# Stages that hand work from engine to engine are put further apart in a two-layer attention and GLU kernel

## The chip, the cores and the metric

The kernel runs on one core of a Trainium2 chip. The metric is the device time of one execution in microseconds; before the change its median over three runs is 2419.47 us (2416.88 to 2425.47). A core has five engines that run beside each other and wait for one another through semaphores: TensorE (PE, matrix products; PEld is its weight load), VectorE (DVE), ScalarE (ACT), GpSimd (POOL) and SyncE (SP, which here only issues DMAs). Each engine takes its instructions in the order in which the program put them in its queue.

## What is computed

One sequence of 2048 rows of 448 values passes through attention, GLU, attention, GLU, each with a layer norm ahead of it and a residual sum behind it. Attention has 16 query heads of 28 values and one shared key and value head.

```python
def _A_ref(x, wq, wk, wv, wo):
    q = (x @ wq).reshape(B, S, H, Dh).transpose(0, 2, 1, 3)
    k = x @ wk
    v = x @ wv
    scores = jnp.einsum("bhqd,bkd->bhqk", q, k) * (Dh ** -0.5)
    p = _softmax(scores, axis=-1)
    o = jnp.einsum("bhqk,bkd->bhqd", p, v)
    return o.transpose(0, 2, 1, 3).reshape(B, S, H * Dh) @ wo

def _B_ref(x, w_gate, w_up, w_down):
    h = _sigmoid(x @ w_gate) * (x @ w_up)
    return h @ w_down

x = x + _A_ref(_layernorm(x), ...)      # layer 0
x = x + _B_ref(_layernorm(x), ...)
x = x + _A_ref(_layernorm(x), ...)      # layer 1, same weights
x = x + _B_ref(_layernorm(x), ...)
```

## The kernel before

Most operands are split into two f16 parts, a high and a low one, so that products of f16 tiles keep more digits: ACT writes the high part as a cast, and DVE or POOL writes what the cast left out. Such a pair is always ACT first, then DVE or POOL.

**Units and steps.** A layer's queries are 16 units of 128 rows. A unit has 16 steps, one for each 128 keys (`kt`). One step of the loop at L904 places, by the string ORDER (L888, `XFSFSFSFSPM`): a tick of the side stages (X); four times a slice of filler work and a score product (F, then S: L494, followed by ACT's exponential P at L497); the four products with the values of the step before (P: `pv`, L505); and one group of the next unit's maxima (M). M is four products `mx` (L477), each reduced by DVE to one column (`mp`, L481). 16 such groups make a unit's row maxima (20 for layer 1's first unit), and the maxima run three groups ahead, so the last group of the next unit stands at step 12 of 16.

**The maxima's transpose.** After the last group `row_max` (L447) lets DVE make `m` (L451, L452). A later function `fin` transposes it on PE (`mt`, L457), DVE copies it (`mr`, L459), and SP stores it into a row of QS (L460), which the next unit's scores read. `fin` is deferred by LAG slices of filler (L409); four slices are a step. `defer(fn, lag)` puts a function on a list that is looked through at each slice and whenever a PSUM tile for filler is taken.

**Side stages.** `later(...)` hangs up a chain of stages, each with the number of ticks since the one before; a tick comes once in a step (X). Each finished unit runs the chain f0, fx, fy, fz, fw, fa, fb, fc (L547 to L609): the sums of the softmax go out to DRAM and come back laid out anew, DVE takes reciprocals (fy), they go out and come back copied over partitions into `lb` (fw: four DMAs of SP, L574), POOL multiplies (fa, L579), ACT and DVE split the product into `oT` (fb, L585 and L586), and fc hangs up the product with WO (L596). Then x1 and its statistics (L601), the normed row (fd: DVE `xn` L318, DVE's cast L310, POOL's low part L311 and L312), its DMA transpose (fe, L322) and ff. Two units form a block; when ff has run for both, the block's GLU work is added to the filler.

**Filler.** `bulk` (L642) is a block's GLU: seven times a gate product `gp`, tanh on ACT (`th`, L656), an up product `up`, then DVE's `th` (L664), ACT's high part of `h` (L667) and DVE's low part (L668); then the products with WD (`dn`, L693). How much filler a slice takes follows from `rate` (L927 to L931): the work left over the steps until step 48 + 32n, with n the blocks whose GLU has been added. In the last rounds of a layer (L942) a tick is followed by four slices of 450 ns of filler by the kernel's own estimate (VS, L892).

**Next layer's rows.** In layer 0, `down` makes x2 and its statistics, and then hangs up db, dc, dd, de, df: db (L709) makes the normed row with `ln_split` (DVE `xn`, ACT's cast L310, DVE's low part L311 and L312), dc transposes it by DMA, dd makes keys and values, de transposes the keys, df counts them. `xn` has one buffer, shared by fd and db.

**Banks.** `mx`, `s`, `mt` and all filler products share seven PSUM banks in rotation; PE can take a bank again only when DVE or ACT has read what was in it.

Of the kernel before, what the change touches and what calls it, by code (L numbers as in the profile page):

```python
# [8 lines left out]
F32 = mybir.dt.float32  # L9
F16 = mybir.dt.float16  # L10
I32 = mybir.dt.int32
AF = mybir.ActivationFunctionType
OP = mybir.AluOpType
# [6 lines left out]
def interleaved_layers_kernel(ctx: ExitStack, tc: tile.TileContext, x, wq, wk, wv, wo, wg, wu, wd, out, layers=2):  # L20
# [6 lines left out]
    nc = tc.nc  # L27
    _, S, D = x.shape
# [4 lines left out]
    TB, WB, HB = 2, 4, 10  # L33
# [8 lines left out]
    wk1 = ctx.enter_context(tc.tile_pool(name="wk1", bufs=2))  # L42
# [23 lines left out]
    def defer(fn, lag=0):  # L66

        pend.append((now[0] + lag, fn))
# [246 lines left out]
    def ln_split(xt, mean, r, eng=nc.vector, xn=None, hi=nc.vector.tensor_copy):  # L315
        if xn is None:
            xn = wk1.tile([128, D], F32, name="xn", bufs=1)
        nc.vector.tensor_scalar(xn, xt, mean, r, op0=OP.subtract, op1=OP.mult)  # L318
        return hilo(xn, eng, hi)
# [86 lines left out]

    QS, QH, PVS = {}, {}, {}
    stored = set()
    LAG = 4  # L409
    KEYS = {False: [0, 512, 1024, 1536, 2048], True: [0, 512, 1024, 1536, 1792, 2048]}  # L410

    def parts_of(l, u):
# [98 lines left out]


    XTQ, BLK = {}, {}
    side = []

    def later(*stages):

        side.append([stages[0][0], list(stages)])

    def tick():  # L520

        for s in list(side):
            s[0] -= 1
            if s[0] <= 0:
                flush()
                fill.run(s[1].pop(0)[1]())
                if s[1]:
                    s[0] = s[1][0][0]
                else:
                    side.remove(s)  # L530

    class Block:
# [8 lines left out]
        def tile(self, u):  # L541

            l, b = self.l, self.b
            t = u % TB
            v = {}

            def f0():  # L547
                v["o"] = PVS.pop((l, u))
                nc.sync.dma_start(sums[u % 2], v["o"][28:128:32])
                v["xr"] = wk1.tile([128, D], F32, tag="xr", name="xr", bufs=4)  # L550
                nc.sync.dma_start(v["xr"], x[0, u * 128:(u + 1) * 128] if l == 0 else x2d[u])
                return
                yield

            def fx():
                v["rc"] = wk1.tile([128, 16], F32, name="rc")
                nc.sync.dma_start(v["rc"], sums[u % 2].rearrange("g (a b) -> (g a) b", b=16))
                return
                yield

            def fy():
                nc.vector.reciprocal(v["rc"], v["rc"])
                return
                yield

            def fz():
                nc.sync.dma_start(sums[u % 2].rearrange("g (a b) -> (g a) b", b=16), v["rc"])
                return
                yield

            def fw():
                lb = v["lb"] = wk1.tile([128, 512], F32, name="lb", bufs=1)
                for g in range(G):
                    nc.sync.dma_start(lb[32 * g:32 * g + 32], sums[u % 2][g:g + 1].to_broadcast([32, 512]))  # L574
                return
                yield

            def fa():
                nc.gpsimd.tensor_tensor(v["lb"], v["o"], v["lb"], op=OP.mult)  # L579
                return  # L580
                yield

            def fb():
                oT = v["oT"] = wk1.tile([128, 2, 512], F16, name="oT")
                nc.scalar.copy(oT[:, 0], v["lb"])  # L585
                defer(lambda: nc.vector.tensor_tensor(oT[:, 1], v["lb"], oT[:, 0], op=OP.subtract))  # L586
                return
                yield

            def wo_gen():  # L590
                need(1)
                p = fps([128, D], F32, "wo")
                n = 0
                for h in range(4):
                    for a, c in ((0, 0), (0, 1), (1, 0)):
                        nc.tensor.matmul(p, v["oT"][:, a, h * 128:(h + 1) * 128], WO[:, c, h], start=n == 0, stop=n == 11)  # L596
                        n += 1
                        yield C448

                def f():  # L600
                    nc.vector.scalar_tensor_tensor(self.x1[:, t], p, osc, v["xr"], op0=OP.mult, op1=OP.add)  # L601
                    v["ls"] = ln_stats(self.x1[:, t])[0]
                defer(f)
                later((2, fd), (3, fe), (2, ff))

            def fc():
                fill.urgent.append(wo_gen())
                return
                yield  # L609

            def fd():
                if t == TB - 1:
                    self.load_w(0)
                    self.load_w(1)
                v["hl"] = ln_split(self.x1[:, t], *v["ls"], eng=nc.gpsimd)
                return
                yield

            def fe():
                if t == 0:  # L620
                    self.XT2 = wk1.tile([128, 7, TB * 128], F16, name="XT2")
                t7_dma(v["hl"], self.XT2, t)
                return
                yield

            def ff():
                self.fed += 1
                if self.fed == TB:
                    fill.add(self.bulk(), BULK)
                    if b == NBL - 1 and not self.last:  # L630
                        for n in (1, 2):
                            fill.add(qgen(l + 1, n), G * QCH)
                return
                yield
            return (1, f0), (1, fx), (1, fy), (1, fz), (1, fw), (1, fa), (1, fb), (2, fc)

        def load_w(self, f):
            need(2 + f)
# [3 lines left out]
        def bulk(self):  # L642
            l, b, XT2 = self.l, self.b, self.XT2
            hs = []

            def glu(f):
# [15 lines left out]
                def ev():  # L662
                    t = th
                    nc.vector.scalar_tensor_tensor(t, th, 1.0, up.rearrange("p j n -> p (j n)"), op0=OP.add, op1=OP.mult)  # L664

                    def parts():
                        nc.scalar.activation(h[:, 0], t, AF.Copy, scale=2.0 ** -17)  # L667
                        defer(lambda: nc.vector.scalar_tensor_tensor(h[:, 1], t, 2.0 ** -17, h[:, 0], op0=OP.mult,  # L668
                                                                     op1=OP.subtract), 1)
                    defer(parts, 2)  # L670
                defer(ev)
                hs.append(h)

# [9 lines left out]
        def down(self, t, hs):  # L683
# [23 lines left out]
            defer(ev)  # L707

            def db():  # L709
                v["hl"] = ln_split(v["x2"], *v["ls"], eng=nc.vector, hi=nc.scalar.copy)  # L710
                return
                yield

# [20 lines left out]
                yield  # L734
            if not self.last:
                v["XT"] = XTQ[l + 1, u // 4]
                later((2, db), (3, dc), (2, dd), (2, de), (2, df))

    QCH = 11 * C512
    BULK = FC * 22 * C256 + TB * 3 * FC * C448  # L740
# [144 lines left out]
        k += 1  # L885

    early[0] = False
    ORDER = "XFSFSFSFSPM"  # L888
    MORE = (5, 10)
    FIRST = KT * TB + 16  # L890
    KEEP = 28000
# [1 line left out]
    for l in range(layers):  # L893
# [10 lines left out]
        for step in range(U * KT):  # L904
            u, kt = divmod(step, KT)
            P = []
            for o in ORDER:
                if o == "S":
                    scores(l, u, kt, len(P), P)
# [63 lines left out]
```

## Time and profile before

| | |
|---|---|
| median of 3 runs | 2419.47 us |
| profiled execution | 2419.03 us, span 2417.3 us |
| granted clock of TensorE, mean | 0.978 |
| busy: PE, DVE, ACT, POOL | 2250.9, 1627.5, 1573.6, 329.0 us |
| score products `s`, `pv`, `mx` (PE) | 2048, 4096, 2064 instructions |
| exponentials P (ACT) | 2048, 1322.4 us |
| reduces mp (DVE) | 2064, 1270.9 us |

Rows of the profile read: engine, source line, operation, output <- inputs, a count or a shape. In a timeline a row begins with its start and length in us and may end with the idle time of the engine before it and what ended it. In a list of waits a row gives the engine and line that waited, what it waited for, and then the total in us, the number of times and the longest. In a table of stretches each engine has busy us and, in brackets, its instructions; behind them stand the granted clock, the DMA share and GB/s. PE's ends are modelled, so a busy PE is not PE at its peak.

### The profile page before, as it was taken

The page shows a single profiled execution, that of the slowest core. Times are in us where ns is not written, and L with a number is a line of the kernel's source. Part 1 is how long each engine was busy: PE and PEld are TensorE (multiplying, and loading weights), DVE is VectorE, ACT ScalarE, POOL GpSimd, SP SyncE. Part 2 cuts the span into 40 slices and gives each one's busy share as a digit, 9 for nine tenths or more (in the row PEclk, how much of TensorE's full clock was granted, in tenths as well). Part 3 has the DMA queues.
Part 4 walks back from the last instruction along what each step waited for, and adds up shares of the span by engine and source line. Part 5 has one row for each costly group of instructions (what it writes and reads, how often), then busy time and mean ns, then how long its engine had stood idle before and what let it go on. Part 6 is the DMA issues. An engine that isn't in the chain of part 4 may idle for free.

```text
span 2417.3 us, 40904 instructions
## 1 busy us (share of the span) xinstructions
PE 2250.9 (93%) x15608; PEld 994.7 (41%) x15608; DVE 1627.5 (67%) x2874; ACT 1573.6 (65%) x2583; POOL 329.0 (14%) x589
## 2 busy tenths in 40 slices
PE   3788899999999999999999989999999999999999
PEld 1211244343444444344564213434344444444356
DVE  3776768777767777776266987767777777767421
ACT  5386767676667767666712877767676767767751
POOL 5402546100100010001011000000000000000010
PEclk9798899999999999999999999999999999999999
DMA  5433454321223233231452011323131222322133
GB/s 144 130 100 85 148 186 138 90 88 54 86 75 101 74 90 94 59 94 47 127 155 77 13 45 59 108 57 89 51 101 61 92 74 82 91 80 84 63 100 124
DMA packets 227524, 218.57 MB, mean 90 GB/s; under 512 B 159408, under 2 KB 187760, under 8 KB 227328
## 3 DMA queue, kind: packets, MB, share of 16 engines
q1 hardware_dynamic: 221856, 200.24, 28.4%
q0 software_dynamic: 4352, 14.74, 1.7%
q8 instruction: 122, 2.00, 0.3%
q10 hardware_dynamic: 1120, 0.98, 0.1%
q14 instruction: 74, 0.61, 0.1%
HBM read 175.37 MB, written 23.59 MB: 82 GB/s over the span
## 4 chain that ended last, share of the span: by engine, by line
PE 75%; DVE 13%; DMA 3%; ACT 2%; SPq 2%; issue 2%; POOL 2%; ACTq 0%; DVEq 0%; POOLq 0%
PE pv L505 18%; PE s L494 15%; PE gp L334 10%; PE up L334 10%; DVE mp L481 10%; PE dn L693 9%; PE mx L477 6%; PE wo L596 3%; PE qp L334 2%; ACT P L497 2%; DMA XT<-hl 1%; SPq L424 1%; DMA lb<-sums 1%; SPq L574 0%; DMA wgu<-wgu_d 0%
## 5 line engine op out<-in xcount | busy, mean ns | idle before, releaser
L497 ACT ACTIVATE P<-s,esc 128x512 f32<-128x512 f32 x2048 | 1322.4, 690 | 477.2 <-PE s L494 452.6
L481 DVE TENSOR_REDUCE mp<-mx 128x1 f32<-128x512 f32 (+1 forms) x2064 | 1270.9, 679 | 468.3 <-PE mx L477 465.6
L494 PE MATMUL s<-QS,KK 96*128 96x512 f16 x2048 | 762.9, 387 | 33.4 <-DVE mp L481 23.0
L505 PE MATMUL pv<-P,VV 128*32 128x512 f32 x4096 | 558.6, 617 | 0.0
L334 PEld LDWEIGHTS <-wgu 128*128 128x128 f16 x4928 | 457.5, 97 | 239.1 <-issue 91.8
L334 PE MATMUL up<-XT,wgu 128*128 128x256 f16 x2464 | 370.6, 273 | 1.8 <-DVE mp L481 1.8
L334 PE MATMUL gp<-XT,wgu 128*128 128x256 f16 x2464 | 369.5, 274 | 2.7 <-DMA wgu<-wgu_d 2.3
L693 PE MATMUL dn<-WD,h 128*128 128x448 f16 x1344 | 319.7, 353 | 0.0
L494 PEld LDWEIGHTS <-KK 96*128 96x128 f16 x2048 | 193.7, 98 | 162.9 <-issue 82.9
L477 PE MATMUL mx<-KK,QH 32*128 32x512 f16 (+1 forms) x2064 | 232.4, 392 | 28.3 <-ACT P L497 18.1
L477 PEld LDWEIGHTS <-QH 32*128 32x128 f16 x2064 | 56.6, 91 | 454.2 <-issue 450.2
L693 PEld LDWEIGHTS <-h 128*128 128x128 f16 x1344 | 123.0, 97 | 138.5 <-issue 27.7
L579 POOL TENSOR_TENSOR lb<-pvs,lb 128x512 f32<-128x512 f32 x32 | 40.5, 1267 | 1000.5 <-DMA lb<-sums 833.1
L505 PEld LDWEIGHTS pv<-P,VV 128*32 128x32 f32 x4096 | 81.9, 109 | 205.8 <-issue 194.9
L667 ACT ACTIVATE h<-th 128x512 f16<-128x512 f32 x112 | 70.4, 628 | 93.5 <-DVE th L664 93.5
L664 DVE SCALAR_TENSOR_TENSOR th<-th,up 128x512 f32<-128x512 f32 x112 | 75.9, 678 | 63.9 <-PE up L334 51.9
L668 DVE SCALAR_TENSOR_TENSOR h<-th,h 128x512 f16<-128x512 f32 x112 | 77.0, 687 | 47.0 <-ACT h L667 47.0
L295 POOL TENSOR_SCALAR rs<-mv 128x1 f32<-128x1 f32 (+2 forms) x53 | 12.2, 230 | 676.9 <-DVE mv L290 666.1
L656 ACT ACTIVATE th<-gp,gsc 128x512 f32<-128x512 f32 x112 | 76.7, 684 | 39.8 <-PE gp L334 39.6
L334 PE MATMUL qp<-XT,WQ 128*128 128x512 f16 x352 | 100.4, 415 | 1.8 <-DVE mp L481 1.2
L596 PE MATMUL wo<-WO,oT 128*128 128x448 f16 x384 | 93.6, 355 | 0.4 <-DVE mp L481 0.4
L334 PEld LDWEIGHTS <-WQ 128*128 128x128 f16 x352 | 33.9, 104 | 54.3 <-issue 26.9
(116 smaller groups left out, 766.3 us busy)
## 6 DMA issues: line engine op xcount, KB each, us to landing
wgu<-wgu_d SPq DMA_DIRECT2D x224, 512.0 KB
QS<-qd SPq DMA_DIRECT2D x384, 32.0 KB
lb<-sums SPq DMA_DIRECT2D x128, 64.0 KB
xr<-in_A_x_dram SPq DMA_DIRECT2D x32, 224.0 KB
qd<-qst POOLq DMA_DIRECT2D x28, 256.0 KB, 2.7
wgu_d<-sgu POOLq DMA_DIRECT2D x14, 512.0 KB, 3.8
QH<-qd SPq DMA_DIRECT2D x28, 128.0 KB
x2d<-x SPq DMA_DIRECT2D x16, 224.0 KB
```

Source lines behind the costliest of these rows:

```text
L334: nc.tensor.matmul(ps, a, b, start=n == 0, stop=n == 10)
L477: nc.tensor.matmul(ps[h][:, :k1 - k0], qh[32 * h:32 * h + 32, g], KK[l][32 * h:32 * h + 32, 1, k0:k1], start=True, stop=True, tile_positio ...
L481: nc.vector.tensor_reduce(mp[:, g, h, kb:kb + 1], ps[h][:, :k1 - k0], axis=AX.X, op=OP.max)
L494: nc.tensor.matmul(s, KK[l][0:96, 0, kt * 128:(kt + 1) * 128], QS[l, u][:, g].rearrange("p h n -> p (h n)"), start=True, stop=True)
L497: nc.scalar.activation(p, s, AF.Exp, scale=esc)
L505: nc.tensor.matmul(v[32 * g:32 * g + 32], VV[l][:, kt], P[g], start=kt == 0, stop=kt == KT - 1, tile_position=(0, 32 * g))
L596: nc.tensor.matmul(p, v["oT"][:, a, h * 128:(h + 1) * 128], WO[:, c, h], start=n == 0, stop=n == 11)
L656: defer(lambda: nc.scalar.activation(th, gp.rearrange("p j n -> p (j n)"), AF.Tanh, scale=gsc))
L664: nc.vector.scalar_tensor_tensor(t, th, 1.0, up.rearrange("p j n -> p (j n)"), op0=OP.add, op1=OP.mult)
L667: nc.scalar.activation(h[:, 0], t, AF.Copy, scale=2.0 ** -17)
L668: defer(lambda: nc.vector.scalar_tensor_tensor(h[:, 1], t, 2.0 ** -17, h[:, 0], op0=OP.mult, op1=OP.subtract), 1)
L693: nc.tensor.matmul(p, hs[f // 2][:, a, o:o + 128], WD[:, f, c], start=n == 0, stop=n == 3 * FC - 1)
```

## The change

Five edits stand further apart what passes between engines; nothing in the arithmetic changes. LAG goes from 4 to 7 slices. The stage fb comes two ticks behind fa instead of one, and DVE's low part of `oT` two more slices behind ACT's. ACT's high part of `h` comes four slices behind DVE's `th` instead of two. db is cut into db (DVE `xn`), db2 (ACT's cast) and db3 (DVE's low part), one tick apart, and dc follows two ticks after db3. Since `xn` now stays in use between ticks, a set `held` keeps every fd and db back while it does. ORDER becomes a list of two strings, which are alike.

```diff
-    LAG = 4
+    LAG = 7
...
-    side = []
+    side, held = [], set()
...
             s[0] -= 1
+            if s[1][0][1].__name__ in ("fd", "db") and held:
+                s[0] = max(s[0], 1)
             if s[0] <= 0:
...
-                defer(lambda: nc.vector.tensor_tensor(oT[:, 1], v["lb"], oT[:, 0], op=OP.subtract))
+                defer(lambda: nc.vector.tensor_tensor(oT[:, 1], v["lb"], oT[:, 0], op=OP.subtract), 2)
...
-            return (1, f0), (1, fx), (1, fy), (1, fz), (1, fw), (1, fa), (1, fb), (2, fc)
+            return (1, f0), (1, fx), (1, fy), (1, fz), (1, fw), (1, fa), (2, fb), (2, fc)
...
-                    defer(parts, 2)
+                    defer(parts, 4)
...
             def db():
-                v["hl"] = ln_split(v["x2"], *v["ls"], eng=nc.vector, hi=nc.scalar.copy)
+                mean, r = v["ls"]
+                xn = v["xn"] = wk1.tile([128, D], F32, name="xn", bufs=1)
+                held.add("xn")
+                nc.vector.tensor_scalar(xn, v["x2"], mean, r, op0=OP.subtract, op1=OP.mult)
+                return
+                yield
+
+            def db2():
+                v["hl"] = wk1.tile([128, 7, 128], F16, name="hl", bufs=2)
+                nc.scalar.copy(v["hl"].rearrange("p c j -> p (c j)")[:, 0:448], v["xn"])
+                return
+                yield
+
+            def db3():
+                f, src = v["hl"].rearrange("p c j -> p (c j)"), v["xn"]
+                nc.vector.tensor_tensor(f[:, 448:512], src[:, 384:448], f[:, 384:448], op=OP.subtract)
+                nc.vector.tensor_tensor(f[:, 512:896], src[:, 0:384], f[:, 0:384], op=OP.subtract)
+                held.discard("xn")
...
-                later((2, db), (3, dc), (2, dd), (2, de), (2, df))
+                later((2, db), (1, db2), (1, db3), (2, dc), (2, dd), (2, de), (2, df))
...
-    ORDER = "XFSFSFSFSPM"
+    ORDERS = ["XFSFSFSFSPM", "XFSFSFSFSPM"]
...
+            ORDER = ORDERS[(l, 0) in BLK and BLK[l, 0].fed == TB]
```

How this moves instructions shows at three places. The first is DVE around a unit's row maxima in the steady part of layer 1 (m is made at L451 and L452, mr is the copy of the transpose, mp are the reduces of the next maxima). Before, and then with the change:

```order
L481 TENSOR_REDUCE mp_18117<-mx 128x1 x4
L451 TENSOR_REDUCE m_18934<-mp_18117 128x16
L452 TENSOR_SCALAR m_18935<-m_18934 128x16
L459 COPY mr<-mt 16x128
L481 TENSOR_REDUCE mp_18975<-mx 128x1 x12
```

```order
L481 TENSOR_REDUCE mp_18100<-mx 128x1 x4
L451 TENSOR_REDUCE m_18922<-mp_18100 128x16
L452 TENSOR_SCALAR m_18923<-m_18922 128x16
L318 TENSOR_SCALAR xn<-x_17452,mv,rs 128x448
L310 CAST hl<-xn 128x448
L481 TENSOR_REDUCE mp_18969<-mx 128x1 x4
L459 COPY mr<-mt 16x128
L481 TENSOR_REDUCE mp_18969<-mx 128x1 x8
```

The copy mr, and with it PE's transpose mt, now stands behind the next step's four reduces, and the normed row of fd (xn, hl), which stood ahead of m, behind it.

The second is ACT around the attention output of a unit early in layer 1 (P are the exponentials, pvs the copy of the finished `pv`, th and h the GLU's). Before, and then with the change:

```order
L509 COPY pvs<-pv 128x512
L497 ACTIVATE P<-s,esc 128x512 x16
L656 ACTIVATE th<-gp,gsc 128x512
L497 ACTIVATE P<-s,esc 128x512 x8
L585 CAST oT<-lb 128x512
L667 ACTIVATE h<-th 128x512
```

```order
L509 COPY pvs<-pv 128x512
L497 ACTIVATE P<-s,esc 128x512 x19
L658 ACTIVATE th<-gp,gsc 128x512
L497 ACTIVATE P<-s,esc 128x512 x9
L587 CAST oT<-lb 128x512
L497 ACTIVATE P<-s,esc 128x512
L669 ACTIVATE h<-th 128x512
```

The cast that needs POOL's product stood behind 24 exponentials of the unit and now stands behind 28, one step later.

The third is DVE where layer 0 makes the next layer's normed row (fd's xn is that at L318, db's the one that reads x2, called x_6479 and x_6473 here; the low parts are hl at 128x64 and 128x384). Before, and then with the change:

```order
L452 TENSOR_SCALAR m_6531<-m_6530 128x16
L459 COPY mr<-mt 16x128
L481 TENSOR_REDUCE mp_6570<-mx 128x1 x4
L318 TENSOR_SCALAR xn<-x_6479,mv,rs 128x448
L311 TENSOR_TENSOR hl<-xn,hl 128x64
L312 TENSOR_TENSOR hl<-xn,hl 128x384
```

```order
L452 TENSOR_SCALAR m_6519<-m_6518 128x16
L318 TENSOR_SCALAR xn<-x_4995,mv,rs 128x448
L310 CAST hl<-xn 128x448
L481 TENSOR_REDUCE mp_6564<-mx 128x1 x4
L715 TENSOR_SCALAR xn<-x_6473,mv,rs 128x448
L459 COPY mr<-mt 16x128
L481 TENSOR_REDUCE mp_6564<-mx 128x1 x8
L727 TENSOR_TENSOR hl<-xn,hl 128x64
L728 TENSOR_TENSOR hl<-xn,hl 128x384
```

db's low part stood directly behind xn and now stands two steps of reduces later, with ACT's cast in between; and fd's xn, whose reader is POOL, now stands only four reduces ahead of db's xn.

## The prediction

> **What bounds the kernel now.** I read the page first, then busy time by stage, then what TensorE (PE) waits for in each stage, then single places in the timeline. The page's busy shares, and a table of stages (span, then busy us of PE, PEld, DVE, ACT and POOL, then granted clock, DMA share, GB/s):
>
> ```profile
> PE 2250.9 (93%) x15608; PEld 994.7 (41%) x15608; DVE 1627.5 (67%) x2874; ACT 1573.6 (65%) x2583; POOL 329.0 (14%) x589
> ...
> 130.00:345.00 215.00, 179.32 (x1020) 50.71 (x1018) 157.47 (x271) 156.25 (x269) 72.56 (x72) 0.89 0.43 129
> 345.00:1198.00 853.00, 825.20 (x5891) 373.04 (x5889) 588.72 (x1034) 591.17 (x957) 112.13 (x221) 1.00 0.30 87
> 1198.00:1331.80 133.80, 127.18 (x909) 74.91 (x907) 81.80 (x160) 31.62 (x59) 18.97 (x45) 1.00 0.38 116
> 1331.80:1487.50 155.70, 137.70 (x808) 32.14 (x811) 130.72 (x225) 118.71 (x199) 7.97 (x18) 0.92 0.10 27
> 1487.50:2285.00 797.50, 780.80 (x5592) 353.80 (x5595) 565.38 (x967) 559.78 (x879) 49.82 (x108) 1.00 0.27 79
> 2285.00:2417.30 132.30, 128.45 (x953) 82.54 (x945) 28.51 (x46) 51.96 (x84) 7.98 (x18) 0.99 0.36 117
> ```
>
> The stages are the start of layer 0's attention, its steady part, the hand-over between the layers, the first three units of layer 1, its steady part, and the tail. PE leads everywhere, so a gain can only come out of PE's idle time: 35.7, 27.8, 6.6, 18.0, 16.7 and 3.9 us in these stages (span less busy), 109 us together. The first 130 us are preparation, which the change does not reach. In the two start stages little filler work exists; DVE is busy 84% of the time from 1331.8 to 1487.5 and PE's clock falls to 0.89 and 0.92. What ends PE's waits, in the order of those stages (first, second, fourth, fifth):
>
> ```profile
> PE mt L457 <- DVE m L452: 6.9, 3, 2.6
> PE mx L477 <- ACT P L497: 7.7, 3, 3.8
> ...
> PE mt L457 <- DVE m L452: 11.5, 12, 1.8
> PE mx L477 <- ACT P L497: 5.6, 22, 0.6
> ...
> PE mt L457 <- DVE m L452: 8.4, 3, 3.0
> PE mx L477 <- ACT P L497: 4.7, 2, 2.6
> ...
> PE mt L457 <- DVE m L452: 10.5, 12, 1.1
> PE s L494 <- ACT P L497: 2.1, 5, 0.4
> ```
>
> Two things stand out: every unit's transpose of the maxima (mt) waits for DVE, and PE waits for exponentials (P) that ACT delivers late.
>
> **The transpose, LAG 4 to 7.** One steady unit, PE then DVE:
>
> ```profile
> 1666.07 0.38 PE L494 MATMUL s<-QS,KK 96*128 96x512 f16 x1
> 1667.51 0.22 PE L457 MATMUL mt<-id,m 128*16 128x128 f16 x1 [1.06 <-DVE m L452]
> ...
> 1664.51 2.48 DVE L481 TENSOR_REDUCE mp<-mx 128x1 f32<-128x512 f32 x4
> ...
> 1667.29 0.17 DVE L452 TENSOR_SCALAR m<-m 128x16 f16<-128x16 f32 x1
> 1667.77 0.21 DVE L459 COPY mr<-mt 16x128 f16<-16x128 f16 x1 [0.31 <-PE mt L457]
> 1669.85 1.29 DVE L481 TENSOR_REDUCE mp<-mx 128x1 f32<-128x512 f32 x2 [1.86 <-PE mx L477]
> ```
>
> PE comes 1.06 us before DVE has finished m, although DVE is not behind afterwards: it then idles 0.31 and 1.86 us. Three slices later means one score, one pv group, one mx group and two more slices with filler: about three quarters of a 4.1 us step, some 3 us, well over 1.06. So the wait goes in the 24 steady units: 11.5 + 10.5 = 22.0 us. I take 20, because PE then runs into DVE's other work now and then. Bounds: 0 (DVE is simply met later) and 22. What comes late next is the row's way into QS: copy, DMA, first score of the next unit. It loses some 3 us and keeps a step and more, so I cost it at nothing; if that cover were gone PE would wait in each unit, at s instead of mt.
>
> **Attention output one step later.** A start unit of layer 1 (SP's issues, POOL, ACT, PE):
>
> ```profile
> 1386.11 5.18 SPq L424 DMA_DIRECT2D QS<-qd  x11
> 1391.34 1.82 SPq L574 DMA_DIRECT2D lb<-sums  x4
> ...
> 1394.98 1.25 POOL L579 TENSOR_TENSOR lb<-pvs,lb 128x512 f32<-128x512 f32 x1 [68.34 <-DMA lb<-sums]
> 1396.27 0.62 ACT L585 CAST oT<-lb 128x512 f16<-128x512 f32 x1 [3.48 <-POOL lb L579]
> ...
> 1397.52 0.37 PE L477 MATMUL mx<-KK,QH 32*128 32x512 f16 x1 [2.11 <-ACT P L497]
> ...
> 1440.00:1456.00 16.00, 13.25 (x67) 2.88 (x66) 11.18 (x19) 10.25 (x18) 1.26 (x1) 0.81 0.37 112
> ```
>
> The QS loads sit ahead of lb in SP's queue, so lb lands late, ACT stands still 3.48 us in front of the cast, every exponential behind it is late, and PE has no bank for mx. The next unit does the same, and the table over it (last row) has the clock at 0.81. The three places where ACT is held, over the whole run:
>
> ```profile
> ACT h L667 <- DVE th L664: 93.5, 69, 4.6
> ACT hl L310 <- DVE xn L318: 68.9, 14, 15.5
> ACT oT L585 <- POOL lb L579: 33.9, 15, 4.6
> ```
>
> The change puts the cast a step later (2.5 us without filler, about 4 with), the h copy two slices later, and the normed row's cast a step behind the xn that it reads. Against means of 2.3, 1.4 and 4.9 us a wait that covers nearly all of the first two and most of the third. PE sees only a part: in the steady stages 5.6 + 2.1 = 7.7 us (bounds 0 and 7.7; I take 6). DVE's own lags (subtract of oT, h, hl) move along with their ACT parts and lie beside the reduces, at nothing.
>
> **The start stages together.** Direct waits are 6.9 + 7.7 = 14.6 us in layer 0 and 8.4 + 4.7 = 13.1 in layer 1. DVE bounds the second: it idles 25.0 of 155.7 us, so no more than 25 can go. I take 15 in each, 30 in all, a little over the direct waits since the smaller ones and the low clock come on top, between 0 and 63 (25.0 in layer 1; 14.6 and the clock's loss, 0.11 x 215 = 23.7, in layer 0).
>
> The rows above show the clock low only in the stages with the long waits. The Trainium skill, TensorE: Matmul & The Clock Gate, Part 1, has a rule for it: a window of about 3.4 us without enough work puts the array at half rate until a busy window has passed. The trace agrees as to where it happens, and by that rule the waits cost more than themselves, which is a rival below.
>
> **What it adds.** First, every stage behind the cast is a step later, so a block's GLU work becomes available at step 50 + 32n instead of 49 + 32n, while the rate of filling still aims at 48: one more step without filler for 7 blocks in each layer, 14 steps. Such steps, four in a row and then one at a hand-over:
>
> ```profile
> 1331.80:1341.70 9.90, 9.83 (x65) 2.25 (x65) 9.90 (x17) 9.03 (x16) 0.00 (x0) 1.00 0.07 17
> ...
> 1613.61 0.38 PE L494 MATMUL s<-QS,KK 96*128 96x512 f16 x1 [0.23 <-DVE mp L481]
> ...
> 1669.40:1673.50 4.10, 4.10 (x40) 2.15 (x36) 3.08 (x5) 1.92 (x4) 0.00 (x0) 1.00 0.84 193
> ```
>
> A step without filler takes 2.47 us at DVE's pace, and PE loses 0.23 in it; the filler comes back in the other 31 steps, where PE is the bound (4.10 of 4.10 us, DVE 3.08). 14 x 0.23 = 3 us; nothing if DVE has caught up, all of it, 14 x 2.47 = 35 us, if the fuller steps are no longer PE's. I take 3.
>
> Second, the tails. The last block's rows come one round of 1.8 us of filler later:
>
> ```profile
> 1237.21 1.28 SPq L322 DMA_TRANSPOSE XT<-hl  x1
> 1240.15 0.46 PE L334 MATMUL kv<-WKV,XT 128*128 128x56 f16 x11 [2.19 <-DMA XT<-hl]
> ...
> 2348.07 2.43 PE L596 MATMUL wo<-WO,oT 128*128 128x448 f16 x12
> 2357.13 1.28 SPq L322 DMA_TRANSPOSE XT<-hl  x1
> 2363.77 2.46 PE L334 MATMUL gp<-XT,wgu 128*128 128x256 f16 x21
> ```
>
> A DMA transpose releases its reader 2.94 us after the issue (1237.21 to 1240.15). At the end that gives 2360.1 against gp at 2363.8: 3.7 us of cover for 1.8. Between the layers up to 1.8 us may show; I take 1.
>
> Third, xn has one buffer. The block's normed row is now read by POOL one step, not two, before db writes xn again. POOL begins the lower half 1.06 us after DVE's cast and needs 0.30 + 0.91, 2.3 us, and four reduces of 2.48 us stand between in DVE's order: covered. If not, DVE waits up to 2.3 us in about 7 units of layer 0, 16 us. I take 1. The guard that holds fd and db back only acts while xn is held, three ticks out of 32, and the order shows one db moved by it or by its block. ORDERS holds the same order twice: no cost.
>
> **Sum.** 20 + 6 + 30 - 3 - 1 - 1 = 51 us. The profiled execution took 2419.0 us, its span being 2417.3, and the median is 2419.5, so 0.4 us of difference is left aside: **2368 us**.
>
> **Rivals.**
> 1. The wait moves to DVE. Freed of mt, PE meets DVE at the next banks, since later GLU rows, x1 statistics (0.68 + 0.63 + 0.18 us) and mr can fall into one step. For it: DVE's 84% in layer 1's start, and PE already waits there for reduces. Against: the 1.86 us of DVE idling behind mr. Half the steady terms, 13, and 13 of the starts, less 5: 21 us, 2398.
> 2. The clock gives more. If the half-rate stretches go, the starts yield what they can: 25 + 30 instead of 30, so 76 us, 2343. For it: 0.81 around the long wait. Against: DVE and ACT would have to keep up. The skill's page named above is this case's rule.
> 3. Slower: the dry steps. If the 31 fuller steps meet DVE or ACT as their bound, the 14 empty ones are lost whole, 35 us, with both tails at 1.8 each, 39 us. This decides as soon as the rest brings less than 39: with rival 1's gains before its costs, 26, it is 13 us slower, 2432. Against: the 1.02 us that DVE has free in the 4.10 us step.
> 4. Nothing: the waits were there only because PE had time, or the mt wait reappears at s before the next unit; 2417.
>
> **How the numbers follow.** A run of this kernel can be told from no change at about 0.3%, 7 us. Chances: forecast (2355 to 2385) 0.60, rival 1 0.19, rival 2 0.10, rival 3 0.05, rival 4 0.06. Faster by over 0.3%: the first three, less a little of rival 1's far end, 0.87; same 0.08; slower 0.05. The range takes in rivals 1 and 2, 2340 to 2402; it leaves out rivals 3 and 4 and the far ends.
>
> **What would show it.** Right: mt waits for m nearly gone in all but each layer's first unit, ACT's waits before oT and hl down to a few us, PE's clock near 1 from 1330 on, the first three units of layer 1 some 15 us shorter. Wrong: PE waits for s or mx on DVE that grow by as much; 14 hand-over steps that cost over 1 us each; PE waiting for QS<-mr or DVE for POOL before xn.

## The result, and the profile after

| | before | after |
|---|---|---|
| median (4 runs each) | 2418.28 us (2416.88 to 2425.47) | 2335.44 us (2334.41 to 2339.73) |
| ratio | | 0.9655, 95% interval 0.9632 to 0.9678 |
| profiled execution | 2419.03 us, span 2417.3 | 2334.43 us, span 2332.6 |
| granted clock, mean | 0.978 | 0.990 |

The change makes the kernel 83 us faster. The forecast was 51 us, to 2368, and the time lies 4.6 us below the low end of its range. The direction held, and so did the mechanisms; the price of the waits did not.

The page of the changed kernel, its busy times and the head of its chain:

```profile
span 2332.6 us, 40912 instructions
...
PE 2215.7 (95%) x15608; PEld 989.4 (42%) x15608; DVE 1623.6 (70%) x2874; ACT 1575.4 (68%) x2583; POOL 329.9 (14%) x589
...
PE 84%; DVE 7%; DMA 3%; ACT 2%; SPq 2%; issue 1%; POOL 1%; ACTq 0%; DVEq 0%; POOLq 0%
```

As many instructions on PE, DVE and ACT as before; the chain goes through PE for 84% (before 75%) and through DVE for 7% (before 13%). Note that PE is busy for 35 us less than before with the same 15608 instructions. Some 14 us of that lie in the start of layer 0, where the clock rose as well. What is left, above all in the steady parts, is the clue to what the prediction missed.

To compare stages of two executions, I cut both at the same score products. The first table has the changed kernel from the score that stood at 130 us before: the start of layer 0, its steady part (to the end of unit 14), unit 15 with the hand-over, layer 1's first three units, its units 3 to 14. Columns as in the prediction's table. Then the first, second and fifth stage of the kernel before.

```profile
127.12:321.50 194.38, 165.66 (x1011) 47.68 (x1010) 155.81 (x269) 153.31 (x264) 67.88 (x69) 0.96 0.45 134
321.50:1089.50 768.00, 759.80 (x5487) 343.10 (x5484) 577.81 (x1016) 550.89 (x884) 111.74 (x210) 1.00 0.32 90
1089.50:1274.68 185.18, 178.66 (x1295) 102.92 (x1292) 87.82 (x175) 71.65 (x125) 24.61 (x60) 0.98 0.41 117
1274.68:1413.46 138.78, 131.68 (x795) 31.32 (x794) 128.41 (x222) 118.26 (x196) 8.01 (x18) 0.97 0.12 31
1413.46:2191.01 777.55, 773.84 (x5573) 350.95 (x5569) 570.49 (x977) 557.46 (x877) 49.94 (x108) 1.00 0.27 81
```

```profile
130.12:345.89 215.77, 180.09 (x1022) 51.15 (x1021) 157.35 (x271) 157.00 (x270) 72.56 (x72) 0.88 0.43 130
345.89:1143.55 797.66, 769.86 (x5475) 344.65 (x5474) 577.84 (x1013) 545.31 (x879) 106.59 (x206) 1.00 0.29 84
...
1481.23:2276.72 795.49, 778.66 (x5572) 351.35 (x5569) 571.65 (x977) 558.79 (x877) 49.82 (x108) 1.00 0.26 79
```

The starts get 21.4 and 17.1 us shorter, the steady parts 29.7 and 17.9. Look at layer 0's steady part: PE's idle time (length less busy) falls from 27.8 to 8.2 us, by 19.6, but the stage gets 29.7 us shorter. The other 10.1 us come out of PE's busy time, with as many instructions (some 5480) at a clock of 1.00 in both. So part of what the records call busy was waiting.

What ends PE's waits over the whole run, in the kernel before and then in the changed one:

```profile
PE mt L457 <- DVE m L452: 38.2, 32, 3.0
...
PE s L494 <- DVE mp L481: 23.0, 77, 0.8
PE mx L477 <- ACT P L497: 18.1, 27, 3.8
```

```profile
PE kv L334 <- DMA XT<-hl: 29.5, 14, 8.7
PE s L494 <- DVE mp L481: 23.9, 83, 0.8
...
PE mt L457 <- DVE m L452: 2.5, 3, 1.0
PE mt L457 <- ACT P L497: 2.1, 2, 1.5
...
PE mx L477 <- ACT P L497: 1.6, 6, 0.6
```

The transpose's wait for m fell from 38.2 to 2.5 us, and mx waits 1.6 us for ACT's exponentials instead of 18.1. The score's wait for DVE's reduces is what it was (23.0, now 23.9): the waits have not moved there. A steady unit's transpose, first PE and SP, then DVE:

```profile
1598.54 0.22 PE L457 MATMUL mt<-id,m 128*16 128x128 f16 x1
1599.99 0.56 SPq L460 DMA_DIRECT2D QS<-mr  x1
...
1595.83 0.17 DVE L452 TENSOR_SCALAR m<-m 128x16 f16<-128x16 f32 x1
1597.37 2.48 DVE L481 TENSOR_REDUCE mp<-mx 128x1 f32<-128x512 f32 x4
1599.76 0.20 DVE L459 COPY mr<-mt 16x128 f16<-16x128 f16 x1
```

m is ready at 1596.00, 2.5 us before PE comes for it, and PE goes straight on. And the start unit of layer 1 that the prediction showed around 1386 to 1398, now (SP's issues, POOL, ACT, PE):

```profile
1333.06 5.60 SPq L424 DMA_DIRECT2D QS<-qd  x12
1338.70 1.82 SPq L576 DMA_DIRECT2D lb<-sums  x4
...
1342.25 1.26 POOL L581 TENSOR_TENSOR lb<-pvs,lb 128x512 f32<-128x512 f32 x1 [67.73 <-DMA lb<-sums]
1343.54 0.62 ACT L587 CAST oT<-lb 128x512 f16<-128x512 f32 x1 [0.90 <-POOL lb L581]
...
1344.40 0.88 PE L477 MATMUL mx<-KK,QH 32*128 32x512 f16 x4
```

lb lands as late as before, behind the QS loads, but ACT stands still for 0.90 us in front of the cast instead of 3.48, and the row of mx that followed a wait of 2.11 us follows none. Yet this row of four products is 0.88 us long and an undisturbed one 0.39: it holds some 0.5 us of waiting that no list of waits shows.

### The profile page after: what moved, and what is told of

The parts are those of the page before. It is cut to its first block, busy times and chain, and to the rows that moved or that the text cites. A ratio compares the mean times of both kernels' runs of the same rounds, so it can differ in the third digit from the quotient of the medians.

```text
span 2332.6 us, 40912 instructions
## 1 busy us (share of the span) xinstructions
PE 2215.7 (95%) x15608; PEld 989.4 (42%) x15608; DVE 1623.6 (70%) x2874; ACT 1575.4 (68%) x2583; POOL 329.9 (14%) x589
## 4 chain that ended last, share of the span: by engine, by line
PE 84%; DVE 7%; DMA 3%; ACT 2%; SPq 2%; issue 1%; POOL 1%; ACTq 0%; DVEq 0%; POOLq 0%
PE pv L505 20%; PE s L494 17%; PE gp L334 12%; PE up L334 12%; PE dn L695 11%; DVE mp L481 6%; PE mx L477 6%; PE wo L598 3%; PE qp L334 2%; DMA XT<-hl 1%; ACT P L497 1%; SPq L424 1%; DMA wgu<-wgu_d 0%; PE kv L334 0%; DMA xr<-in_A_x_dram 0%
## 5 line engine op out<-in xcount | busy, mean ns | idle before, releaser
L494 PE MATMUL s<-QS,KK 96*128 96x512 f16 x2048 | 751.8, 383 | 38.8 <-DVE mp L481 23.9
L505 PE MATMUL pv<-P,VV 128*32 128x512 f32 x4096 | 550.7, 610 | 1.1 <-ACT pvs L509 1.1
L477 PE MATMUL mx<-KK,QH 32*128 32x512 f16 (+1 forms) x2064 | 220.3, 387 | 11.3 <-DVE mp L481 4.7
L670 DVE SCALAR_TENSOR_TENSOR h<-th,h 128x512 f16<-128x512 f32 x112 | 77.8, 695 | 40.8 <-ACT h L669 40.7
L334 PE MATMUL qp<-XT,WQ 128*128 128x512 f16 x352 | 95.6, 400 | 1.7 <-ACT qf L383 0.9
```

Source lines behind the costliest of these rows:

```text
L334: nc.tensor.matmul(ps, a, b, start=n == 0, stop=n == 10)
L477: nc.tensor.matmul(ps[h][:, :k1 - k0], qh[32 * h:32 * h + 32, g], KK[l][32 * h:32 * h + 32, 1, k0:k1], start=True, stop=True, tile_positio ...
L494: nc.tensor.matmul(s, KK[l][0:96, 0, kt * 128:(kt + 1) * 128], QS[l, u][:, g].rearrange("p h n -> p (h n)"), start=True, stop=True)
L505: nc.tensor.matmul(v[32 * g:32 * g + 32], VV[l][:, kt], P[g], start=kt == 0, stop=kt == KT - 1, tile_position=(0, 32 * g))
```

## The experiments

Three theories stood at first. **A**: each edit takes away its own waits, independently, and these cost more than PE's idle rows show. **B**: the gain beyond the idle rows comes from the clock, since short stretches without work put PE at half rate. **C**: the edits need each other, so one alone brings little. All kernels below compute the same as the two of the comparison; only places and lags differ. Those of the first three sets were run once each, with the kernel before beside them.

### Each edit alone, on the kernel before

```diff
s_lag
-    LAG = 4
+    LAG = 7
s_out
-                defer(lambda: nc.vector.tensor_tensor(oT[:, 1], v["lb"], oT[:, 0], op=OP.subtract))
+                defer(lambda: nc.vector.tensor_tensor(oT[:, 1], v["lb"], oT[:, 0], op=OP.subtract), 2)
-            return (1, f0), (1, fx), (1, fy), (1, fz), (1, fw), (1, fa), (1, fb), (2, fc)
+            return (1, f0), (1, fx), (1, fy), (1, fz), (1, fw), (1, fa), (2, fb), (2, fc)
s_row (with db, db2, db3 and held as in the change)
-                later((2, db), (3, dc), (2, dd), (2, de), (2, df))
+                later((2, db), (1, db2), (1, db3), (2, dc), (2, dd), (2, de), (2, df))
s_glu
-                    defer(parts, 2)
+                    defer(parts, 4)
```

> The kernel before with LAG 7 alone. Theory A (each edit takes away its own waits, and PE's waits cost about 0.2 us more apiece than the idle rows show, since a matmul's modelled end lies behind its issue): 30 waits of about 1.06 to 3 us, 37 us by the rows and some 43 with the hidden part; about 1.1 to 1.3 us less in every steady unit of both layers, 2377. Theory B (the waits mattered by the half-rate clock that followed them): little in the steady units, most of the gain in the first three units of each layer, 2395. Theory C (the edits need each other, since DVE or ACT would only be met later): under 20 us, 2400.

> The kernel before with fb one tick later and the subtract of oT two slices later, nothing else. Theory A: the long stalls of units 1 to 3 of layer 0 and 1 and 2 of layer 1 go, 4 to 6 us each, and about 1.5 us in each odd steady unit of layer 0, nothing in layer 1's steady units; 14 drier steps cost 3 us: 30 us in all, 2389. Theory B: 15 us more in the start units than the direct waits of 13 us. Theory C: under 10 us, because mt is then met by the same backlog.

> The kernel before with db cut into three ticks (and the guard), nothing else. Theory A: about 2.5 us for each block of layer 0 and nothing in layer 1: 12 to 18 us, 2402. By the prediction's own rows it would be at most 5 us, 2413. Theory C: no change.

> The kernel before with the h copy four slices behind DVE instead of two, nothing else. Theory A: about 1 us in each odd steady unit of layer 1, less in layer 0: 8 to 12 us, 2408. If the h copy only waits where ACT has time anyway: no change, 2418.

Measured, beside 2417.33 us of the kernel before: s_lag 2378.97, s_out 2376.49, s_row 2400.24, s_glu 2414.70; gains of 38.4, 40.8, 17.1 and 2.6 us. By stage, in the profiled executions cut at the same scores (us gained on the kernel before's first profile):

| stage | after | s_lag | s_out | s_row | s_glu |
|---|---|---|---|---|---|
| preparation (to 130 us) | 3.0 | -0.2 | 0.1 | 0.1 | 0.4 |
| layer 0, start | 21.4 | 7.5 | 14.2 | -1.6 | -0.2 |
| layer 0, steady | 29.7 | 12.4 | 15.4 | 16.6 | 0.8 |
| unit 15 and hand-over | -3.4 | 0.0 | -2.1 | 3.2 | -0.5 |
| layer 1, units 0 to 2 | 17.1 | 9.2 | 9.4 | 0.5 | -1.1 |
| layer 1, steady | 17.9 | 11.2 | 6.5 | 0.0 | 5.3 |
| unit 15 and tail | -1.1 | 0.0 | -0.8 | 0.0 | -0.3 |

Two edits alone bring 38 and 41 us, so C falls. B cannot be the main cause: the steady parts run at 1.00 in all of these and hold 47.6 of the 84.6 us. A holds in its first part, that each edit ends waits of its own (over the run, mx still waits 19.5 us for P in s_lag, and mt 34.6 us for m in s_out). It does not hold in that they are independent: the single gains add to 98.9 us, more than the change brings, so they overlap. In layer 1's steady part, where PE's list had 2.1 us of waits for P, s_glu alone brings 5.3 us, and s_out 6.5, where theory A expected nothing.

The steady part of layer 0 in s_out, by stage and by PE's waits:

```profile
331.58:1113.87 782.29, 762.84 (x5488) 343.45 (x5485) 578.68 (x1016) 548.76 (x884) 110.89 (x211) 1.00 0.30 89
```

```profile
PE mt L457 <- DVE m L452: 8.8, 12, 1.2
PE mx L477 <- ACT P L497: 4.5, 15, 0.7
PE s L494 <- ACT P L497: 2.8, 8, 0.5
PE s L494 <- DVE mp L481: 2.5, 11, 0.2
```

The stage is 15.4 us shorter than before, while the row that I had priced the edit by, mx waiting for P, only falls from 5.6 to 4.5 us. PE's busy time again falls, by 7.0 us (769.86 to 762.84). Where this sits is seen in the kernel before at a late cast (first a normal group of mx, then ACT, then the disturbed group):

```profile
476.56 0.39 PE L477 MATMUL mx<-KK,QH 32*128 32x512 f16 x4
...
480.31 0.62 ACT L585 CAST oT<-lb 128x512 f16<-128x512 f32 x1 [2.47 <-POOL lb L579]
480.84 2.42 ACT L497 ACTIVATE P<-s,esc 128x512 f32<-128x512 f32 x4
...
480.83 0.39 PE L477 MATMUL mx<-KK,QH 32*128 32x512 f16 x1
481.57 0.37 PE L477 MATMUL mx<-KK,QH 32*128 32x512 f16 x1 [0.36 <-ACT P L497]
482.15 0.53 PE L477 MATMUL mx<-KK,QH 32*128 32x512 f16 x2 [0.21 <-ACT P L497]
```

Four mx on their own row groups start almost together and take 0.39 us in all. Here each gets its bank when ACT, held up for 2.47 us, has read an exponential out of it. They start at 480.83, 481.57 and 482.15, and the fourth some 0.16 us later (the last row holds two, 0.53 us in place of a lone one's 0.37): nearly 1.5 us from first to last. The idle rows show 0.36 + 0.21 = 0.57. The rest is hidden under the modelled length of each lone mx.

So I took the distance from start to start of each pair of neighbouring products, less the usual distance of the same pair (the lowest fifth of its values in the kernel before; for mt, which nearly always waited there, the 0.31 us that it takes in the changed kernel), as the time lost. Differences of up to 0.01 us are left out. What remains of a stage should then be the same work in all kernels:

| steady part | length | lost | remains | PE idle (length less busy) |
|---|---|---|---|---|
| layer 0, before | 797.7 | 49.6 | 748.0 | 27.8 |
| layer 0, s_lag | 785.2 | 37.0 | 748.3 | 16.6 |
| layer 0, s_out | 782.3 | 33.3 | 749.0 | 19.5 |
| layer 0, after | 768.0 | 19.3 | 748.7 | 8.2 |
| layer 1, before | 795.5 | 28.3 | 767.2 | 16.8 |
| layer 1, after | 777.5 | 10.3 | 767.2 | 3.7 |

It is, within 1 us in layer 0 and exactly in layer 1. (How small differences are counted moves the column of losses by up to 5 us, for all kernels alike; what remains stays equal among them.) So there were 78 us to lose in the two steady parts, where the idle rows had 44.6. Before a product mx, 16.5 us were lost in layer 0 before and 3.6 after, against 5.6 before in the rows of mx there. This is the other part of A, that the waits cost more than the idle rows, and it is shown.

### Each edit put back, on the changed kernel

```diff
m_lag
-    LAG = 7
+    LAG = 4
m_out
-            return (1, f0), (1, fx), (1, fy), (1, fz), (1, fw), (1, fa), (2, fb), (2, fc)
+            return (1, f0), (1, fx), (1, fy), (1, fz), (1, fw), (1, fa), (1, fb), (2, fc)
m_row (db in one piece again)
-                later((2, db), (1, db2), (1, db3), (2, dc), (2, dd), (2, de), (2, df))
+                later((2, db), (3, dc), (2, dd), (2, de), (2, df))
m_glu
-                    defer(parts, 4)
+                    defer(parts, 2)
```

In m_out the lag of oT's subtract goes back as well.

> The changed kernel with LAG back at 4. If the terms add up (theory A): the loss equals what LAG 7 alone gained, about 40 us, 2375, with 1.2 us more in every steady unit. If the edits need each other (theory C): a loss of over 50 us.

> The changed kernel with fb and the subtract of oT put back. Theory A: 25 to 30 us lost, nearly all in units 1 to 3 of layer 0 and 1 and 2 of layer 1, and the handover between the layers and the tail 2 to 4 us shorter; 2362. Theory C: over 40 us lost.

> The changed kernel with db in one piece again (fd is no longer held). Theory A: 12 to 18 us lost, all in layer 0, about 2.5 us in each odd unit; 2350. By the prediction's rows: 5 us, 2340.

> The changed kernel with the h copy two slices behind DVE again. Theory A: 5 to 10 us lost, in the odd steady units, 2343. Otherwise no change, 2335.

Measured, beside 2415.87: m_lag 2371.95, m_out 2355.66, m_row 2334.15, m_glu 2340.37. Without LAG the change is worth 43.9 us, without the later attention output 60.2, without the cut db 81.7, without the later `h` 75.5. The last differs by 4.4 us in the preparation, which this edit does not reach, so little of it is the edit's. By stage, in us lost against the first profile of the changed kernel (which has no run in this set):

| stage | m_lag | m_out | m_row | m_glu |
|---|---|---|---|---|
| preparation (to 130 us) | 2.9 | 3.1 | 0.4 | 4.4 |
| layer 0, start | 11.9 | 13.8 | -1.0 | -1.0 |
| layer 0, steady | 6.2 | -1.5 | 2.5 | 1.3 |
| unit 15 and hand-over | -1.9 | -4.8 | -2.2 | 1.1 |
| layer 1, units 0 to 2 | 8.3 | 8.3 | -0.2 | 0.3 |
| layer 1, steady | 9.7 | 3.0 | 0.0 | 0.0 |
| unit 15 and tail | 0.3 | -0.8 | 0.3 | -0.4 |

So in the changed kernel the later attention output is worth its time in the starts. In the steady parts, where it had brought 21.9 us alone, taking it away costs only 1.5: the other edits cover it there. In the whole time m_row loses nothing, a surprise, since db cut alone had brought 17 us. ACT's wait for xn, which the cut is there to end, is still in m_row's units (ACT's waits, 345 to 1140 us):

```profile
ACT hl L310 <- DVE xn L318: 35.4, 11, 3.5
```

ACT stands still for 35 us, against 0.4 us in the same stretch of the changed kernel, and the stage is only 2.5 us longer (4.0 for the same pair in the last set). What covers the rest is not shown.

### Why the cut of db brings 17 us alone: queue or wait

SP's queue in the unit with the late cast shown above, four rows in a row of the kernel before (XT is dc's transpose, KK de's). Then s_row's:

```profile
466.07 6.50 SPq L424 DMA_DIRECT2D QS<-qd  x12
472.67 1.21 SPq L366 DMA_TRANSPOSE KK<-ktl  x1
473.92 1.29 SPq L322 DMA_TRANSPOSE XT<-hl  x1
475.25 1.97 SPq L574 DMA_DIRECT2D lb<-sums  x4
```

```profile
465.32 6.26 SPq L424 DMA_DIRECT2D QS<-qd  x12
471.63 1.82 SPq L576 DMA_DIRECT2D lb<-sums  x4
473.54 1.21 SPq L366 DMA_TRANSPOSE KK<-ktl  x1
474.85 1.24 SPq L322 DMA_TRANSPOSE XT<-hl  x1
```

The cut moves dc, and the stages hung behind it, a tick later, and so lb goes ahead of two transposes, 2.5 us of the queue. Theory **Q** says that this order is the gain; theory **H** says that it is ACT's wait for xn. One kernel has only the later tick, one only the cut, with dc's tick kept. In the same unit lb goes ahead of the two transposes in p_dc4 and stays behind them in p_row1, as meant.

```diff
p_dc4
-                later((2, db), (3, dc), (2, dd), (2, de), (2, df))
+                later((2, db), (4, dc), (2, dd), (2, de), (2, df))
p_row1 (with db, db2, db3 and held)
-                later((2, db), (3, dc), (2, dd), (2, de), (2, df))
+                later((2, db), (1, db2), (1, db3), (1, dc), (2, dd), (2, de), (2, df))
```

> The kernel before with dc, the DMA transpose of the next layer's rows, one tick later and db still in one piece. Theory Q (what the cut of db gained alone is a matter of SP's queue: dc then stands behind lb's four DMAs instead of ahead of them, so lb lands earlier and ACT waits less for it): about 2.5 us less in each odd unit of layer 0 from unit 5 on, 2402. Theory H (it is ACT's wait for xn and DVE's wait for the cast that the cut removes): no change, 2417.

> The kernel before with db cut into three ticks, but dc one tick after db3, so that it keeps its old tick and its old place ahead of lb in SP's queue. Theory Q: next to nothing, at most 0.5 us an odd unit, 2414. Theory H: the whole gain of the cut, 2.5 us an odd unit, 2402.

Measured, beside 2421.00: p_dc4 2402.67, p_row1 2411.99. In the steady part of layer 0, where these edits work, p_dc4 gains 7.3 us and p_row1 1.9, against 16.6 for both together. So the later tick, and with it the queue's order, is the larger single part, the cut alone is close to nothing, and some 7 us need both; what makes these is open. Neither theory holds as it was put. In whole times p_dc4 looks as good as s_row and meets theory Q's 2402, but by luck: 6.8 of its us lie in the start of layer 0, where PE's order of work is the same as before (see the last section). p_row1, whose order on PE is that of before throughout, has 4.6 us there.

### The dry steps and the tails

`FIRST` sets the step that the filler's rate aims at, `KEEP` how much filler, in ns by the kernel's own estimate, is kept from the last block's rate for the rounds after the last unit.

```diff
d_aim
-    FIRST = KT * TB + 16
+    FIRST = KT * TB + 18
d_keep
-    KEEP = 28000
+    KEEP = 30000
```

> The changed kernel with the filling aimed at step 50 + 32n instead of 48 + 32n (FIRST two higher), so that the two steps without filler ahead of each block get some. If the dry steps cost what the rows show, 0.2 to 0.8 us each: 1 us a block, some 10 to 14 us less, 2323. If the filler only changes places: no change, 2335.

> The changed kernel with 2 us more filler kept for the last rounds of each layer (KEEP 30000). If the 3.4 us lost between the layers and the 1.1 us lost at the end come from the chain that is a round longer than the filler: 2 to 4 us less, 2332. If they come from elsewhere (the clock, QS or the weights): no change.

Measured in the same set: d_aim 2343.07, d_keep 2328.87. Aiming later, so that the dry steps get filler, gains nothing in the whole time: its steady parts bring 34.6 + 17.6 us against 29.7 + 17.9 of the change, its hand-over and tail lose 5.5 + 4.7 against 3.4 + 1.1, and the start of layer 0 gains 16.5 against 21.4. Holding back more for the tails looked like a gain and went into the last set.

### Three rounds: which edits carry it, and a faster version

t_after is the changed kernel again; t_two has of the change only LAG and the later attention output; t_row is the changed kernel with db in one piece (m_row's edit); t_keep30 is the changed kernel with KEEP = 30000.

> The changed kernel as it is, beside the next three on the same chip: 2335, half-rate stretches in the preparation moving it by up to 3 us from one execution to the next.

> Only the two edits LAG 7 and fb with the subtract of oT; db in one piece, h copy two slices behind. If the other two edits are already covered by these (their losses alone were 0 and about 0.5 us outside the preparation): within 4 us of the changed kernel, 2336. If they matter together: 2345 or more.

> The changed kernel with db in one piece, timed: within 3 us of the changed kernel, 2335. If the one look was luck and the cut does carry its 17 us: 2350.

> The changed kernel with KEEP 30000, timed: 3 us less than the changed kernel, 2332, from the handover between the layers (2.2 us) and the tail (1.0 us). If the single look was the preparation's clock: the same, 2335.

| 4 runs each | median us | ratio to before (2416.72) | 95% interval |
|---|---|---|---|
| t_after | 2337.26 (2335.00 to 2339.07) | 0.9667 | 0.9652 to 0.9682 |
| t_two | 2337.29 (2337.18 to 2340.34) | 0.9671 | 0.9656 to 0.9686 |
| t_row | 2338.65 (2337.81 to 2339.86) | 0.9673 | 0.9656 to 0.9691 |
| t_keep30 | 2331.40 (2328.56 to 2332.34) | 0.9641 | 0.9626 to 0.9657 |

Two of the edits carry the whole gain, within what the intervals can tell (some 3.5 us). The other edits are not without effect inside: in the profiled executions t_two gains 23.9 us in the steady part of layer 0 and t_after 31.1. But t_after gains less in both starts (20.2 and 14.5 us against 23.5 and 16.8), in the hand-over (-1.9 against -1.1) and in the tail (-1.6 against -0.7). How much of that is the edits' and how much the execution's cannot be split: the start of layer 1 gave 17.1 and 14.5 in two executions of the same kernel.

t_keep30 beats both kernels. It is 5.9 us below t_after, and every one of its runs is below every one of t_after's. Its hand-over loses 1.1 us instead of 1.9, its tail nothing instead of 1.6; these 2.4 us are where the edit works, and the rest lies in stages ahead of it.

## Why the prediction was too small

**What failed is the size of one term: the waits behind ACT in the steady parts, put at 6 us with bounds 0 and 7.7 for the later cast of oT, the later `h` and the cut db together.** On top of LAG they measured 24.0 us there (47.6 less s_lag's 23.6), and without it 31.7 (m_lag, 23.5 + 8.2); the attention output alone made 15.4 + 6.5 = 21.9 (s_out). How the 24.0 divide among the three is open, since each covers for the others: put back one at a time, they cost 1.5, 1.3 and 2.5 us in these parts. The step read the price of ACT being late from the list of PE's waits (5.6 + 2.1 us of rows that name P), and took that for an upper bound. But these rows are idle time between a modelled end and the next start, and a product that waits for a bank in the middle of a group is covered by the modelled length of the one before. Lost from start to start were 49.6 us in the steady part of layer 0, where the prediction saw 27.8. Small rows left out of the sum (in layer 0's steady part kv waiting for XT, 3.2 us, and up waiting for reduces, 1.8) went as well. The same reading stood at the head of the prediction: "a gain can only come out of PE's idle time". That is wrong where the busy time itself shrinks: the steady parts gained 47.6 us, and all of PE's idle time in them was 44.6.

**LAG.** Put at 20 us in the steady parts, with an upper bound of 22.0. s_lag alone measured 12.4 + 11.2 = 23.6. Right, a little over its bound, for the same reason. Put back on the changed kernel it costs 6.2 + 9.7 = 15.9 us there, since the edits overlap. The way into QS stayed at no cost in the steady parts: no wait of s for QS<-mr in them; one of 1.7 us stands at the first unit of layer 1.

**The start stages.** Put at 30 us together, 15 in each, measured 21.4 + 17.1 = 38.5, within the bounds of 0 and 63. The clock rose from 0.88 to 0.96 and, in layer 1, from 0.92 to 0.97, so rival 2's mechanism is likely a part of the gain in the starts; how large a part is not shown. It is not the execution alone: in layer 0's start two profiles of the changed kernel have 0.96 and 0.97, and five of kernels with PE's order of before 0.88 to 0.94. But chance is large here: with that same order the other four of these gain between -1.6 (s_row) and 6.8 us (p_dc4) on the first one, so of the 21.4 us some 7 may be chance.

**The costs.** The dry steps came as told. In the steady parts the kernel before has one short step at each block, 3.07 us from mx to mx; the changed one has that step and a second of 2.86 us (five times, layer 0) or 2.47 (five times, layer 1), and at layer 1's first block a third beside the two of before: eleven in all, the others of the 14 lying in layer 0's start and in each layer's unit 15. What they cost stands within the steady gains above; rival 3, that they are lost whole, did not come, and filling them (d_aim) gained 3.5 to 4.9 us in layer 0's steady part that went again elsewhere. The tails were put at 1 us and cost 1.9 to 3.4 at the hand-over and 1.1 to 1.6 at the end, in two profiles of the changed kernel; that with 3.4 has the clock at 0.98 in the hand-over, that with 1.9 at 1.00. The cover of the last transpose held, since PE waits for no XT there; 0.7 us at the end is pv waiting for ACT's copy, and the rest was not followed up. xn's one buffer was put at 1 us; DVE waited for POOL's reading once, 1.3 us.

**DVE's lags and the other two edits.** The lags cost nothing that shows. ACT's waits in front of hl and h, which the prediction listed beside oT's, carried little time in the changed kernel. They are there now:

```profile
ACT h L669 <- DVE th L666: 49.3, 19, 4.3
...
ACT hl L721 <- DVE xn L715: 27.0, 4, 15.2
...
ACT oT L587 <- POOL lb L581: 9.2, 6, 2.3
```

They fell from 93.5, 68.9 and 33.9. "Down to a few us" holds for oT in the whole run; the 27.0 of hl lie nearly all behind the steady part of layer 0, in which they are 0.4. Of the three it is oT that mattered most in the end: m_out, with 32.0 us of these waits back, is some 20 us slower, and m_row, with 35 us of waits for xn back, is as fast.

**The rivals.** Rival 1, the wait moving to DVE, did not come (23.0 and 23.9 us). Rival 4 neither. Rival 2's 2343 came nearest, but by luck: the clock can be behind the starts alone, not behind the steady parts, where most of the surplus lies.

**Sum, as measured by stage.** Steady parts 47.6 (forecast 20 + 6 - 3 - 1 = 22), starts 38.5 (30), hand-over and tail -4.5 (-1), preparation 3.0 (0; it lay between -1.4 and 3.6 in all executions, though no edit reaches it), together 84.6 us of span.

## What to carry to other kernels

In this kernel a list of waits built from modelled ends was a lower bound for the time that a late reader costs PE; where products of one group take their banks one by one, measure from start to start against the usual distance of the same pair, and see that the remaining work is the same in both kernels. Between two engines in strict order, a step more of distance where the first is sometimes late brought more here than the listed wait that it ends (s_out: 15.4 us in layer 0's steady part, for 5.6 us of mx waiting for P), since exponentials queued behind the waiting cast free their banks late. And an engine's long waits say little of their price: 35 us of ACT's waiting for xn cost 2.5 to 4 us of a stage, the 32 us in front of oT some 20 of the whole. Put each edit back alone to see which carry the gain, since edits that each gain alone may cover for one another.

## What was not expected of the hardware

**PE's busy time of the same work shrinks.** 10.1 us in layer 0's steady part, at the same clock. The Trainium skill, Perfetto Trace Analysis, Tensor Engine Instruction (MATMUL, LD_WEIGHTS), says that the profiler works out a product's end from its size and does not observe it. The rows here agree: a lone mx has 0.37 us (before, at 481.57), though the next one starts only 0.58 us later, and four of them together have 0.39 where nothing holds them up.

**The same order of work gets different clocks.** Layer 0's start, the kernel before and then p_dc4, whose products on PE come in the same order up to 461 us. p_dc4 runs 1.8 us ahead there, so the stretches are of the same work:

```profile
200.00:210.00 10.00, 8.77 (x31) 1.61 (x29) 4.63 (x9) 7.48 (x13) 1.25 (x1) 0.53 0.12 34
```

```profile
198.18:208.18 10.00, 8.36 (x49) 2.77 (x48) 7.20 (x14) 8.22 (x15) 1.25 (x1) 1.00 0.11 32
```

At half rate PE does 31 products in 10 us, where it does 49 at full. From 180 to 240 us the kernel before had 0.81, p_dc4 1.00, and p_dc4's start is 6.8 us shorter. The waits ahead of it are the same in both, none over 0.8 us:

```profile
196.30 0.59 PE L494 MATMUL s<-QS,KK 96*128 96x512 f16 x2 [0.77 <-DVE mp L481]
199.63 0.37 PE L477 MATMUL mx<-KK,QH 32*128 32x512 f16 x1 [0.78 <-DVE mp L481]
```

```profile
194.48 0.59 PE L494 MATMUL s<-QS,KK 96*128 96x512 f16 x2 [0.77 <-DVE mp L481]
197.82 0.37 PE L477 MATMUL mx<-KK,QH 32*128 32x512 f16 x1 [0.78 <-DVE mp L481]
```

The Trainium skill, TensorE: Matmul & The Clock Gate, Part 1, says that the window is free-running, so that the transition varies from run to run. The trace agrees so far: in its record of the granted clock the half-rate stretches of this start last 3.41 us or a whole multiple of it (10.24 us from 200.69 on), and p_dc4, with the same work, has none here. A table of that Part of the Trainium skill also ties the fall to a window of about 3.4 us that is idle; here the clock fell with no idle row over 0.8 us in the 15 us ahead, in one execution and not in another. That many short waits were enough is the likely reading; it is not tested.
